# Loading v of the next attention unit at a unit's second step instead of its fifth

## The chip, the cores and the metric

One Trainium2 chip, one of its cores. The metric is the device time of one execution in microseconds (us). The engines of the core run side by side, each through its own program in order: TensorE (PE: matmuls, and PEld: their weight loads), VectorE (DVE), ScalarE (ACT), GpSimd (POOL) and SyncE (SP). SP, ACT and GpSimd also issue transfers (DMAs), which the core's 16 DMA engines carry out.

## The reference, cut to what matters

```python
def _attn_ref(q, k, v):                    # q, k, v: 4 batches x 12 heads x 448 x 64, float32
    scores = scale * np.matmul(q, k.transpose(0, 1, 3, 2)) - np.log(S)
    attn = 1.0 / (1.0 + np.exp(-scores))   # a sigmoid for each score, no softmax
    return np.matmul(attn, v)

def reference(...):
    x = attn_out.transpose(0, 2, 1, 3).reshape(B * S, H * D)     # 1792 x 768
    h = np.maximum(np.maximum(x @ w1, x @ w2), x @ w3)           # all 768 x 768
    x = h @ w_out
    g = x @ w_in;  g = np.maximum(g, 0) + alpha * np.minimum(g, 0)   # 768 x 2048
    return g @ w_out2                                            # 2048 x 768
```

## The kernel before

The kernel runs the attention first (some 140 us) and then the chain of large matrix products (the function `ff`, all of them issued by the helper on L626). The change touches the attention alone.

**Units and steps.** The function `attention` works in 12 units (`nu`), each of two pairs of heads, z = 0 and z = 1. A unit has seven steps (`NK`, c = 0 to 6). A step issues the scores of one block of 64 keys (`scores`, L506: k against q), after which ACT takes the sigmoid of them into a tile `a` (L514); and, two blocks behind, the product of that tile with v (`av`, L525), summed up in the two PSUM tiles `pav` of the unit (one for each z). The last two blocks of a unit are multiplied with v in step 0 of the next unit; then `to_x` copies the two finished `pav` out, z = 0 on ACT and z = 1 on DVE (L538). So the ACT copy of L538 comes once in a unit, at the end of the unit before.

**Getting k and q ready.** While a unit runs, the next one's k and q are turned (`turn`, called once a step: k of z = 0, k of z = 1, q of z = 0, q of z = 1). In units 1 to 11 the four calls are made at c = 1 to 4, in unit 0 at c = 3 to 6. DVE transposes the loaded rows (L487) in blocks of 32; for k it does so twice, the second time into the tile `side` (L490), and GpSimd then copies four blocks of `side` over into k's tile `kt` (L495, four copies of 32x224 for each z, eight in a unit). The scores of the next unit read `kt`. Each call ends with `load_rows`, in which SP asks for the rows that the same call of the next unit will turn (L467 for k, L474 for q: four loads for each z).

**Getting v.** `load_v` (L448) loads the v of a unit in two transfers of 224 KB, one for each z, into a tile `vt`. There are two such tiles (`bufs=2`), so the v of unit u + 1 takes the place of that of unit u - 1, and its transfer waits until the last `av` of unit u - 1 has read it. Unit 0's v is issued at the start by ACT and SP. All others are issued by GpSimd (L592), at c = 4 of the unit before: there, in GpSimd's program, they stand behind the eight copies of k of that unit (in unit 0, where the turns come later, also behind those of both z). In unit 0, GpSimd also makes a one-column copy into a tile `gate` (L497), which reads `kt`.

**Order.** Each engine's program is written out by hand in the order of the Python calls (the block runs under a manual schedule; waits between engines are put in for the data and the buffers). Between the steps `advance` lets conversions of x and of the weights onto ACT and DVE, by a planner's costs; the change does not touch it.

Of the kernel before, what the change touches and what calls it, by code (L numbers as in the profile page):

```python
# [21 lines left out]
def kernel(  # L22
# [14 lines left out]
    nc = tc.nc  # L37
# [38 lines left out]
    def slot(nm, pool="a", w=TW, dt=F32):  # L76
        if pool == "a":
            pad(pool, 48)
        t = pools[pool].tile([P, w], dt, tag="s" + pool, name=nm, bufs=room[pool])
        if pool != "a":  # L80
            pad(pool, 16)
        return t
# [38 lines left out]
    def load_half(z):  # L121
        if z >= NZ:
            return
        w, kind, m, h = halves[z]
        t = wpool.tile([P, HF, 2], U32, tag="wr", name=f"wr{z}", bufs=4)
        if kind == "col":
            nc.sync.dma_start(
                out=t.rearrange("p (k f) t -> p k (f t)", k=HK),
                in_=w[h * HF : (h + 1) * HF, 2 * m * P : 2 * (m + 1) * P].rearrange(
                    "(k p) f -> p k f", p=P  # L130
                ),
            )
        else:
            c = 2 * 32 * HK
            nc.sync.dma_start(
                out=t.rearrange("p (g f) t -> p g (f t)", g=4),
                in_=w[m * P : (m + 1) * P].rearrange("p (g f) -> p g f", g=4)[
                    :, :, h * c : (h + 1) * c
                ],
            )  # L140
        wraw[z], since[z] = t, tick[0]
# [38 lines left out]
    def advance(cols, act=None, free=False):  # L180
        now[0] += 1
        tick[0] += 1
        loads[0] = max(1, 3 * cols // STEP)
        for e in credit:
            most = cols if e == "D" else 2 * cols // 3 if act is None else act
            credit[e] = min(credit[e] + (cols if act is None else most), most)
        for todo in (urgent, flow):
            n = 0
            while n < len(todo):
                o = todo[n]  # L190
                if (
                    (free or credit.get(o.engine, loads[0] if o.engine == "L" else 1) > 0)
                    and ready(o)
                    and (o.gate is None or o.gate())
                ):
                    emit(o)
                    todo.pop(n)
                else:
                    n += 1
# [187 lines left out]
    def attention(apool, ps_s, ps_v):  # L387
# [8 lines left out]
        n = len(pairs)  # L396
# [51 lines left out]
        def load_v(u, queues):  # L448

            if u >= nu:  # L450
                return
            vts[u] = apool.tile([P, 2, NK, D], F32, tag="vt", name=f"vt{u}", bufs=2)
            for z in range(2):
                b, p = pairs[2 * u + z]
                queues[z].dma_start(
                    out=vts[u][z * KH : (z + 1) * KH].rearrange("r j c d -> r j (c d)"),
                    in_=v[b, 2 * p : 2 * p + 2].rearrange("j (r c) d -> r j (c d)", c=NK),
                )

        def load_rows(u, x, z):  # L460

            if u >= nu:
                return
            b, p = pairs[2 * u + z]
            t = raw[u, x, z] = apool.tile([P, S], F32, tag="raw", name=f"{x}r{2 * u + z}", bufs=6)
            if x == "k":
                nc.sync.dma_start(  # L467
                    out=t, in_=k[b, 2 * p : 2 * p + 2].rearrange("j (r c) d -> (j r) (c d)", c=NK)
                )
                return  # L470
            for j in range(2):
                for h in range(2):
                    p0 = j * D + 32 * h
                    nc.sync.dma_start(  # L474
                        out=t[p0 : p0 + 32].rearrange("p (n d) -> p n d", d=32),
                        in_=q[b, 2 * p + j, :, 32 * h : 32 * h + 32].rearrange(
                            "(n i) d -> i n d", i=32
                        ),
                    )

        def turn(u, x, z):

            if u >= nu:
                return
            t, r = slot(f"{x}t{2 * u + z}"), raw.pop((u, x, z))
            (keys if x == "k" else queries)[u, z] = t
            nc.vector.transpose(out=t, in_=r)  # L487
            if x == "k":
                side = apool.tile([P, S], F32, tag="side", name=f"side{2 * u + z}", bufs=2)
                nc.vector.transpose(out=side, in_=r)  # L490
                to, rows = (y.rearrange("p (c h d) -> p h c d", h=2, d=32) for y in (t, side))
                for j in range(2):
                    for h in range(2):
                        p0, p1 = j * D + 32 * h, j * D + 32 * (1 - h)
                        nc.gpsimd.tensor_copy(to[p0 : p0 + 32, 1 - h], rows[p1 : p1 + 32, h])  # L495
            if u == 1 and (x, z) == ("k", 0):
                nc.gpsimd.tensor_copy(gate[:, :1], t[:, :1])  # L497
            load_rows(u + 1, x, z)

        def scores(u, c):  # L500

            sc = ps_s.tile([P, 2, 512], F32, tag="sc", name=f"sc{u}_{c}")
            for z in range(2):
                for j in range(2):
                    r = slice(j * D, (j + 1) * D)
                    nc.tensor.matmul(  # L506
                        sc[z * KH : (z + 1) * KH, j, :S],
                        keys[u, z][r, c * KH : (c + 1) * KH],
                        queries[u, z][r],
                        start=True,  # L510
                        stop=True,
                    )
            a = at[u, c] = apool.tile([P, 2, S], F32, tag="a", name=f"a{u}_{c}", bufs=5)
            nc.scalar.activation(a, sc[:, :, :S], AF.Sigmoid, bias=bias_s, scale=scale)  # L514

        def av(u, c):

            if c == 0:
                for z in range(2):
                    pv[u, z] = ps_v.tile([P, 512], F32, tag="pv", name=f"pav{u}_{z}")  # L520
            a = at.pop((u, c))
            for z in range(2):
                r = slice(z * KH, (z + 1) * KH)
                for j in range(2):
                    nc.tensor.matmul(  # L525
                        pv[u, z][j * D : (j + 1) * D, :S],
                        vts[u][r, j, c],
                        a[r, j],
                        start=(c == 0),
                        stop=(c == NK - 1),  # L530
                    )

        def to_x(u):

            for z in range(2):
                i = 2 * u + z
                x32[i] = slot(f"x{i}")
                (nc.vector.tensor_copy if z else nc.scalar.copy)(x32[i], pv.pop((u, z))[:, :S])  # L538
                o = Op("A", 0, None, [], None, 1 if u < nu - 1 else 0)
                o.step, o.tick = now[0], tick[0]  # L540
                g, r, c = i // 12, i % 12 // 4, i // 4
                form_ops(
                    f"x{c}", i % 4, range(4 * c, 4 * c + 4), (g, r), xf,
                    lambda g, c, r: "c" if g and r == HK - 1 else "a", lambda pool: True, o,
                )
# [5 lines left out]
        gate = apool.tile([P, 64], F32, tag="gate", name="gate")  # L551
# [20 lines left out]
        for u in range(nu):  # L572
            for c in range(NK):
                scores(u, c)
                if c == 0 and u:
                    for m in (NK - 2, NK - 1):
                        av(u - 1, m)
                    to_x(u - 1)
                elif c > 1:
                    av(u, c - 2)  # L580
                if c == 1 and 1 <= u <= 4:
                    load_half(u - 1)
                if (u, c) == (2, 2):
                    with nc.allow_non_contiguous_dma(reason="a column of slopes per partition"):
                        nc.sync.dma_start(out=alpha_sb, in_=alpha.rearrange("(m p) -> p m", p=P))
                if (u, c) == (5, 0):
                    unit_ops(0, zu[0])
                n = c - (1 if u else 3)
                if 0 <= n < 4:
                    turn(u + 1, *turns[n])  # L590
                if c == 4:
                    load_v(u + 1, (nc.gpsimd, nc.gpsimd))  # L592
                if c == 0:
                    advance(1400, 800)
                elif c != 1:
                    advance(*((600, 450) if c > 2 else (1300, 450)))
# [660 lines left out]
```

## Time and profile before

| | us |
|---|---|
| median of 3 runs | 877.4 |
| lowest and highest of them | 873.63 and 878.9 |
| the profiled execution | 875.98 |
| its span, first to last instruction | 874.2 |
| PE busy in that span | 863.7 (99%) |
| DVE, ACT, POOL busy | 652.4 (75%), 525.3 (60%), 150.8 (17%) |

The profile is of one execution, whose own time is 1.8 us more than its span. A row of the timeline has the start in us from the span's start, how long it took, the engine, the line, the operation and what it writes and reads; in brackets stands how long the engine was idle before it and what it is taken to have waited for. A matmul's end is modelled, so a busy PE can still be slower than it could be; how far it got in a stretch is read from when its work was handed on.

### The profile page before, as it was taken

To read this page: it belongs to the slowest core of one execution; us is meant where nothing else is said; L and a number is where in the kernel's file an instruction comes from. 1 tells how busy PE (TensorE), PEld (TensorE's weight loads), DVE (VectorE), ACT (ScalarE), POOL (GpSimd) and SP (SyncE) were. 2 spreads that over 40 slices of the span, in tenths; PEclk is the share of its full clock that TensorE was granted. 3 is DMA by queue.
4 is the path that set the end of the run, shared out by engine and by line. 5 is a ranking of instruction groups with operands and counts; after the bars stand their busy time and mean duration, and the time that the engine had idled before them with its cause. 6 is when DMAs were issued, how large, how long until landed. Compare 5 with 4: busy or idle time off the path is not lost.

```text
span 874.2 us, 14360 instructions
## 1 busy us (share of the span) xinstructions
PE 863.7 (99%) x5044; PEld 750.9 (86%) x5044; DVE 652.4 (75%) x1261; ACT 525.3 (60%) x1022; POOL 150.8 (17%) x289
## 2 busy tenths in 40 slices
PE   9999999999999999999999999999999999999997
PEld 7645547999999999999999999999999999999997
DVE  3567875899889878787787777777868688768851
ACT  5768987656555554566656677666656655443430
POOL 2444440101101201300000122122121011001211
PEclk9999999999999999999999999999999999999999
DMA  8774740556655655732113433454455999445413
GB/s 208 164 147 110 167 93 22 153 166 219 215 139 171 203 169 140 233 121 73 37 37 104 146 130 129 161 178 157 146 176 188 368 325 365 154 146 162 133 49 64
DMA packets 137224, 137.05 MB, mean 157 GB/s; under 512 B 54752, under 2 KB 127840, under 8 KB 137152
## 3 DMA queue, kind: packets, MB, share of 16 engines
q1 hardware_dynamic: 122448, 93.24, 36.7%
q0 software_dynamic: 12416, 41.86, 14.1%
q10 hardware_dynamic: 2288, 1.03, 0.5%
q8 instruction: 40, 0.66, 0.3%
q14 instruction: 32, 0.26, 0.1%
HBM read 102.28 MB, written 33.82 MB: 156 GB/s over the span
## 4 chain that ended last, share of the span: by engine, by line
PE 92%; DMA 3%; POOL 1%; SPq 1%; DVE 1%; issue 0%; ACT 0%; POOLq 0%; DVEq 0%; ACTq 0%
PE u_0X L626 14%; PE u_1X L626 14%; PE c L626 10%; PE eW L626 10%; PE eX L626 10%; PE u_1W L626 7%; PE u_0W L626 7%; PE pav L525 5%; PE sc L506 4%; PE u_0V L626 4%; PE u_1V L626 4%; PE eV L626 3%; DMA vt<-in_v_dram 3%; POOL kt L495 1%; SPq L474 1%; DMA kr<-in_k_dram 0%
## 5 line engine op out<-in xcount | busy, mean ns | idle before, releaser
L525 PE MATMUL pav<-a,vt 64*64 64x448 f32 x672 | 116.0, 543 | 3.9 <-DMA vt<-in_v_dram 3.3
L506 PE MATMUL sc<-qt,kt 64*64 64x448 f32 x672 | 115.3, 543 | 0.0
L514 ACT ACTIVATE a<-sc,bias_s 128x896 f32<-128x896 f32 x84 | 83.2, 1009 | 24.8 <-PE sc L506 23.7
L525 PEld LDWEIGHTS pav<-a,vt 64*64 64x64 f32 x672 | 51.2, 134 | 34.8 <-issue 22.0
L506 PEld LDWEIGHTS sc<-qt,kt 64*64 64x64 f32 x672 | 52.2, 134 | 25.8 <-issue 22.3
L240 ACT ACTIVATE wt<-wr 128x384 f32<-128x384 f32 x112 | 62.2, 555 | 10.7 <-DMA wr<-in_moe_w_out_dram 9.6
L255 DVE CUSTOM_DVE_ANT_0 wt<-wr,wt 128x768 uint16<-128x768 uint16 x112 | 62.6, 559 | 3.9
L247 DVE SCALAR_TENSOR_TENSOR wr<-wr 128x384 uint32<-128x384 uint32 x112 | 62.2, 556 | 0.6
L243 ACT ACTIVATE wr<-wr 128x384 uint32<-128x384 uint32 x112 | 61.8, 552 | 0.0
L656 DVE SCALAR_TENSOR_TENSOR r<-n,nalpha,r 128x448 f32<-128x448 f32 x64 | 43.4, 682 | 24.5 <-ACT n L653 24.3
L689 POOL DMA_DIRECT2D gd<-r x48 | 26.0, 541 | 198.1 <-DVE r L656 196.9
L495 POOL COPY kt<-side 32x224 f32<-32x224 f32 x88 | 41.3, 469 | 76.6 <-DVE side L490 72.9
L1097 POOL DMA_DIRECT2D out_dram<-o x28 | 17.6, 636 | 167.7 <-DVE o L1092 167.7
L850 POOL DMA_DIRECT2D wd<-wt x32 | 17.4, 544 | 166.7 <-DVE wt L255 146.1
L246 DVE TENSOR_SCALAR wt<-wt 128x384 uint32<-128x384 uint32 x112 | 39.9, 356 | 5.5 <-ACT wt L240 5.5
L759 ACT COPY u<-u_1X 128x448 f32<-128x448 f32 x34 | 18.1, 533 | 29.9 <-PE u_1X L626 29.9
L538 DVE COPY x<-pav 128x448 f32<-128x448 f32 x12 | 7.5, 624 | 37.7 <-PE pav L525 37.7
L746 ACT COPY u_0V<-u_0X 128x448 f32<-128x448 f32 x17 | 8.8, 518 | 42.9 <-PE u_0X L626 42.9
L759 ACT COPY u<-u_0X 128x448 f32<-128x448 f32 x34 | 18.1, 533 | 27.0 <-PE u_0X L626 26.6
L811 ACT COPY y<-c 128x448 f32<-128x448 f32 x24 | 12.8, 534 | 31.6 <-PE c L626 31.6
L294 DVE TENSOR_TENSOR u<-u_0W,u 128x448 f32<-128x448 f32 x28 | 17.4, 622 | 17.3 <-ACT u L759 16.9
L294 DVE TENSOR_TENSOR u<-u_1W,u 128x448 f32<-128x448 f32 x28 | 17.5, 624 | 13.3 <-ACT u L759 8.8
(827 smaller groups left out, 2782.6 us busy)
## 6 DMA issues: line engine op xcount, KB each, us to landing
gl<-gd SPq DMA_DIRECT2D x79, 224.0 KB, 4.2
wr<-in_moe_w_out_dram SPq DMA_DIRECT2D x44, 384.0 KB, 4.2
wr<-in_moe_w_dram SPq DMA_DIRECT2D x36, 384.0 KB, 3.7
wr<-in_moe_w_in_dram SPq DMA_DIRECT2D x32, 384.0 KB, 3.6
wl<-wd SPq DMA_DIRECT2D x64, 192.0 KB, 4.1
gd<-r POOLq DMA_DIRECT2D x48, 224.0 KB, 2.3
gl_T<-gdT SPq DMA_DIRECT2D x32, 224.0 KB, 4.9
wd<-wt POOLq DMA_DIRECT2D x32, 192.0 KB, 3.9
```

The source lines that it names most:

```text
L240: nc.scalar.activation(st["T"].bitcast(F32), st["r"][:, :, 1].bitcast(F32), AF.Abs, scale=2.0**-112)
L243: nc.scalar.activation(st["r"][:, :, 0], st["r"][:, :, 0], AF.Copy, scale=2.0**-29)
L246: nc.vector.tensor_scalar(st["T"], st["T"], 3, None, ALU.logical_shift_left)
L247: nc.vector.scalar_tensor_tensor(out=st["r"][:, :, 0], in0=st["r"][:, :, 1], scalar=0x80000000, in1=st["r"][:, :, 0], op0=ALU.bitwise_and, ...
L255: nc.vector.tensor_tensor(out=st["T"], in0=st["r"][:, :, 0], in1=st["T"], op=ALU.add)
L495: nc.gpsimd.tensor_copy(to[p0 : p0 + 32, 1 - h], rows[p1 : p1 + 32, h])
L506: nc.tensor.matmul(sc[z * KH : (z + 1) * KH, j, :S], keys[u, z][r, c * KH : (c + 1) * KH], queries[u, z][r], start=True, stop=True,)
L514: nc.scalar.activation(a, sc[:, :, :S], AF.Sigmoid, bias=bias_s, scale=scale)
L525: nc.tensor.matmul(pv[u, z][j * D : (j + 1) * D, :S], vts[u][r, j, c], a[r, j], start=(c == 0), stop=(c == NK - 1),)
L626: nc.tensor.matmul(ps[:, : rh.shape[-1]], lt, rh, start=(start and z == 0), stop=(stop and z == len(mms) - 1), skip_group_check=True,)
L656: nc.vector.scalar_tensor_tensor(out=s["r"], in0=s["n"], scalar=nalpha[:, f : f + 1], in1=s["r"], op0=ALU.mult, op1=ALU.add,)
L759: nc.scalar.copy(side[g, k], banks[X][:, :TW])
```

## The change

The v of unit u + 1 is issued by GpSimd at c = 1 of unit u, in front of the turn of k of z = 0, and so in front of all of GpSimd's copies of that unit. For unit 0, the v of unit 1 is issued inside `turn`, after DVE's `side` of the first k and in front of the copies; the one-column copy into `gate` moves there with it and reads `side` instead of `kt`.

```diff
             if x == "k":
                 side = apool.tile([P, S], F32, tag="side", name=f"side{2 * u + z}", bufs=2)
                 nc.vector.transpose(out=side, in_=r)
+                if u == 1 and z == 0:
+                    nc.gpsimd.tensor_copy(gate[:, :1], side[:, :1])
+                    load_v(1, (nc.gpsimd, nc.gpsimd))
                 to, rows = (y.rearrange("p (c h d) -> p h c d", h=2, d=32) for y in (t, side))
                 for j in range(2):
                     for h in range(2):
                         p0, p1 = j * D + 32 * h, j * D + 32 * (1 - h)
                         nc.gpsimd.tensor_copy(to[p0 : p0 + 32, 1 - h], rows[p1 : p1 + 32, h])
-            if u == 1 and (x, z) == ("k", 0):
-                nc.gpsimd.tensor_copy(gate[:, :1], t[:, :1])
             load_rows(u + 1, x, z)
...
                 n = c - (1 if u else 3)
+                if u and n == 0:
+                    load_v(u + 1, (nc.gpsimd, nc.gpsimd))
                 if 0 <= n < 4:
                     turn(u + 1, *turns[n])
-                if c == 4:
-                    load_v(u + 1, (nc.gpsimd, nc.gpsimd))
```

## Rows read from the trace of the kernel before

**Rows 1.** Windows: us; busy us (x count) of PE, PEld, DVE, ACT, POOL; clock; DMA.
```profile
19.91:30.43 10.52, 10.52 (x117) 9.18 (x112) 5.03 (x9) 8.26 (x10) 4.83 (x10) 1.00 0.67 150
30.43:43.07 12.64, 11.26 (x117) 5.47 (x111) 7.72 (x13) 9.19 (x12) 4.95 (x10) 1.00 0.87 180
...
53.59:68.81 15.22, 13.41 (x120) 6.00 (x115) 7.71 (x13) 9.18 (x13) 4.94 (x10) 0.89 0.70 146
...
79.33:90.63 11.30, 11.10 (x120) 5.41 (x115) 8.86 (x17) 10.10 (x17) 4.84 (x10) 1.00 0.82 183
...
101.12:111.97 10.85, 10.81 (x118) 5.41 (x113) 8.82 (x16) 9.54 (x15) 5.30 (x10) 1.00 0.55 124
111.97:123.63 11.66, 11.22 (x120) 5.38 (x115) 9.21 (x16) 9.56 (x14) 4.94 (x10) 1.00 0.62 136
...
134.16:144.40 10.24, 10.24 (x108) 6.60 (x100) 4.01 (x7) 8.16 (x12) 0.00 (x0) 1.00 0.01 2
19.91:144.40 124.49, 120.62 (x1225) 65.73 (x1216) 83.41 (x149) 101.30 (x137) 49.60 (x100) 0.99 0.57 126
144.52:869.29 724.77, 724.77 (x3582) 671.34 (x3582) 563.22 (x1099) 413.54 (x873) 96.09 (x172) 1.00 0.50 161
```

**Rows 2.** Timeline of ACT: first and last of the twelve copies of L538.
```profile
19.91 0.53 ACT L538 COPY x<-pav 128x448 f32<-128x448 f32 x1 [0.39 <-PE pav L525]
...
144.40 0.53 ACT L538 COPY x<-pav 128x448 f32<-128x448 f32 x1 [1.07 <-PE pav L525]
```

**Rows 3.** Timeline of PE: matmuls of L525 that it stood idle for.
```profile
34.28 0.59 PE L525 MATMUL pav<-a,vt 64*64 64x448 f32 x2 [1.29 <-DMA vt<-in_v_dram]
...
56.14 0.97 PE L525 MATMUL pav<-a,vt 64*64 64x448 f32 x4 [0.59 <-DMA vt<-in_v_dram]
58.33 0.59 PE L525 MATMUL pav<-a,vt 64*64 64x448 f32 x2 [1.22 <-DMA vt<-in_v_dram]
...
114.84 0.59 PE L525 MATMUL pav<-a,vt 64*64 64x448 f32 x2 [0.44 <-DVE kt L487]
```

**Rows 4.** The chain that ended last, in unit 1: start, us, what.
```profile
25.79 0.53 POOL vt L455
26.32 7.83 DMA vt<-in_v_dram
34.15 0.14 issue
```

**Rows 5.** The tile vt: from issue to landing, all 24 transfers.
```profile
DMA to landing us min/median/max: 3.2/4.5/7.8
```

**Rows 6.** Windows, as above: the stretch at the lower clock.
```profile
59.29:62.70 3.41, 3.41 (x24) 1.37 (x18) 1.06 (x3) 1.46 (x2) 1.80 (x4) 0.50 0.68 151
```

**Rows 7.** Timeline of POOL: units 0, 1 and 8.
```profile
9.97 1.61 POOL L495 COPY kt<-side 32x224 f32<-32x224 f32 x4 [8.65 <-DVE side L490]
11.64 0.18 POOL L497 COPY gate<-kt 128x1 f32<-128x1 f32 x1
...
13.43 1.32 POOL L455 DMA_DIRECT2D vt<-in_v_dram  x2
21.74 4.05 POOL L495 COPY kt<-side 32x224 f32<-32x224 f32 x8 [6.99 <-DVE side L490]
...
104.72 4.51 POOL L495 COPY kt<-side 32x224 f32<-32x224 f32 x8 [5.60 <-DVE side L490]
```

**Rows 8.** Timeline of PE: the first scores of units 1 and 9.
```profile
17.30 1.11 PE L506 MATMUL sc<-qt,kt 64*64 64x448 f32 x8
...
109.26 0.55 PE L506 MATMUL sc<-qt,kt 64*64 64x448 f32 x2
```

**Rows 9.** DMA issues, 72.0 to 73.6 us, then 75.3 to 77.4: median us to landing.
```profile
qr<-in_q_dram SPq DMA_DIRECT2D x4, 56.0 KB, 2.1
...
qr<-in_q_dram SPq DMA_DIRECT2D x4, 56.0 KB, 5.1
```

**Rows 10.** The tile qr: waits for it, us and times.
```profile
DMA qr<-in_q_dram: 1.5, 2
```

## The prediction, made before the change was run

> **What bounds the kernel now.** I read three views in this order: the waits of PE, a table of windows by unit, and the chain of work that ended last. The table comes first here, because it says how much there is to win. The ACT copy of L538 runs when a unit's last product with v has been handed on, so its twelve starts, from 19.91 to 144.40 [rows 2], cut the attention into eleven periods, and I cut the windows there. From 144.52 to the last matmul PE is busy for 724.77 of 724.77 us [rows 1]: the matrix products behind the attention are PE's alone, without a gap, and what is won in the attention should shift them whole.
>
> An undisturbed period takes 10.52 us; the four periods that have no row share what the others leave of 124.49, which is 42.06 or 10.515 each [rows 1]. It has 14 groups of matmuls (seven of scores, seven of av), so a group takes 10.52/14 = 0.751. The last period ends with the last av instead of going on into a new unit, and has 13 groups: 9.77. Eleven periods without a stall would be 10 x 10.52 + 9.77 = 114.97. They take 124.49 [rows 1]. So **9.5 us** of the attention are lost, and they lie in few periods: 12.64 - 10.52 = 2.12, then 15.22 - 10.52 = 4.70, then 0.78, 0.33, 1.14, and 10.24 - 9.77 = 0.47 in the last.
>
> What they are lost to is seen at PE. Its waits stand at the first av of a unit, and they are for v: 1.29 us before 34.28, then 0.59 and 1.22 in the unit of the 15.22 [rows 3]. The wait of 0.44 before 114.84 is put down to a transpose, but it stands at the same place, the second half of the first av, and I take it for v too. Listed idle time is less than the loss, because a wait for one half of v lets the matmuls of the other half run on alone: PE counts as busy and gets less done. The chain shows why v is late [rows 4]: GpSimd issues it at 25.79 and 26.32, behind its copies of k which began at 21.74 [rows 7]; it takes 7.83 us to land, and PE starts 0.14 after that. So a unit's first av is bound by copies of k, the issue of v, and the landing.
>
> One part of the 4.70 is not a wait: the granted clock is 0.50 from 59.29 to 62.70, that is 1.2 GHz instead of 2.4 [rows 6], right behind the two waits of that unit. Work done at half speed for 3.41 us is some 1.7 us late.
>
> **The change, part by part.**
>
> *v for units 2 to 11, moved to c = 1.* Its two transfers now stand ahead of the eight copies. They still wait for the buffer, which the last av of the unit before frees; that is where the ACT copy of L538 begins, 19.91 in unit 1 [rows 2]. Issuing the pair takes 1.32 in the one row shown [rows 7], so it would be out by 19.91 + 1.3 = 21.2, where it is now begun at 25.79: 5.9 us earlier at its start. The slowest landing of all 24 is 7.83, the median 4.5 [rows 5]. From 20.6, the start of the second transfer, the slowest gives 28.4; the next period begins at 30.43 and av needs v after that. So even the slowest landing has two us to spare, and I cost the wait for v at nothing: 5.9 us more lead hides it. The gain is the whole loss of 9.5, if nothing else is as late.
>
> *What is queued behind it on GpSimd.* The copies of k. They are held by DVE's `side`, not by GpSimd: in unit 1 they begin at 21.74 after 6.99 us idle [rows 7], 1.83 after the period's start. The pair takes 1.32 of that 1.83 and is gone before the copies could begin. In unit 8 they begin at 104.72, 3.6 after the period's start of 101.12. So the cost is nothing as long as the buffer is free within 0.5 us of the ACT copy. If it were freed at the copies' old start instead, each unit's copies would come 1.3 later; that is the upper bound, and it is one of the rivals.
>
> *What is late next.* The copies of k, for the scores of the next unit. In unit 8 they end at 104.72 + 4.51 = 109.23, and the first scores of unit 9 stand at 109.26 [rows 7, 8]: just in time. Without the stall of that period (0.33) those scores would want to start 0.33 sooner. Its bounds are 0 (the copies move with the period, since `side` hangs on the copy of `pav` on DVE) and 0.33. I take 0.3, because the copies start on `side` whether PE stalled behind that point or not.
>
> *v of unit 1, inside `turn`.* Now: four copies from 9.97, the gate copy of 0.18, four more copies, the v pair from 13.43 [rows 7]. Changed: gate copy and pair go first, so the copies end 1.32 + 0.18 = 1.5 us later, at about 13.5 + 1.5 = 15.0. The first scores of unit 1 start at 17.30 [rows 8]: 2.3 us of cover. Without that cover it would cost its 1.5 once. v itself was no one's wait there, so nothing is won.
>
> *DMAs behind the moved ones.* The same bytes go out. But v is now ahead of the q loads of its unit instead of in their midst. Loads of q land in 2.1 us without v beside them and in 5.1 with it [rows 9], so being passed costs a load at most some 3 us. In the whole attention DVE waits for q twice, 1.5 us in all [rows 10], and the scores of unit 1 at 17.30 hide that. From unit 1 on q and k are asked for a unit before they are turned. I cost it at nothing; the other bound is those 3 us once, in unit 0, against no more cover than the copies have there, 2.3: 0.7.
>
> Here a rule speaks against the change. The Trainium skill (DMA: Bandwidth & Descriptors, "Issuing engines are not separate DMA queues") says that transfers from SP, ACT and GpSimd share the same 16 engines and interleave, so a v issued earlier takes from q and k what it gains. The trace agrees that they disturb each other (2.1 against 5.1); what it adds is that the disturbed ones are not awaited.
>
> *The clock.* The fall to 0.50 stands in the one unit with two long waits. With these gone I expect it not to come, and its 1.7 us are part of the 9.5. If it comes anyway, 1.7 stay.
>
> **The sum.** 9.5 lost, less 0.3 that the copies of k may keep: 9.2. Against the profiled execution's own 875.98 that is 875.98 - 9.2 = **866.8**. The median of the runs, 877.4, lies 1.4 higher. I don't carry those 1.4 over: the products behind the attention have no gap in which runs could differ, so runs probably differ in the very stalls that go. If they were carried over it would be 868.2.
>
> **The rivals.**
>
> *B: the copies of k become the bound.* For it: the 0.03 us between copies and scores in unit 8. Against: undisturbed periods exist in the second half too, with the same eight copies, so there the copies are in time for 10.52. If the last six units lose 0.5 each, 3.0 stay: 866.8 + 3.0 = 869.8.
>
> *C: the half-clock stretch comes anyway.* For it: it began behind waits of only 1.22 us, so it may need little. Against: no other such stretch stands in the attention between 19.91 and 144.40 (that window's clock is 0.99 by this one alone). 866.8 + 1.7 = 868.5. The Trainium skill (TensorE: Matmul & The Clock Gate, Part 1) has activity release a throttle that is otherwise the default; by that rule, too, a PE without waits keeps its clock, and the trace agrees in the undisturbed periods (1.00).
>
> *D: the change does nothing.* If the DMA engines are what makes v late, an earlier issue only waits longer. For it: DMA engines are busy 0.87 in the period of the 12.64. Against: they are busy 0.70 in the period that loses most and 0.67 in one that loses nothing [rows 1], and the lead grows by 5.9 us, more than any period loses. Then about 875, within 1%.
>
> *E: GpSimd's wait holds up k (slower).* The v pair now waits for PE in front of the copies. If the buffer were freed so late that the pair ended well after `side`, the copies and then the next scores would be late in unit after unit. It decides once the pair ends later than the 1.83 after the period's start plus what the copies have in hand. With the pair starting only as the copies would have begun, each of the ten units that wait for a buffer loses its 1.32: 866.8 + 13.2 = 880.0, some 0.5% slower; slower by over 1% needs (9.2 + 8.8)/10 = 1.8 a unit. Against: what frees the buffer is the end of the same matmuls that the ACT copy waits for, 1.83 earlier, or for the half of z = 1 a little behind it.
>
> **How the numbers follow.** Forecast 0.62, B 0.15, C 0.08, D 0.08, E 0.07. The forecast's own range is 865.5 (nothing kept, and a little from halves that no longer run apart) to 868.5. With B and C it reaches 870.8 at the upper end, and I take 865 to 871.5: D and E, 0.15 together, are left out. 1% is 8.8 us, about what a measurement of this kernel can tell from no change. The forecast is beyond that by 0.4 counted from the profiled execution and by 1.8 from the median, so I give it 0.52 of its 0.62 as faster by over 1%; of C half, 0.04. E passes 1% on its side with 0.03. So faster 0.56, within 1% 0.41, slower 0.03.
>
> **What would show it.** Right: GpSimd's v pair begins within half a us of the ACT copy of L538 in every unit, with k's copies behind it at the same distance from that copy as before; no wait of PE for vt; eleven periods in 115 to 115.5 us; no row of 0.50 inside the attention; the products behind it still 724.8 us long. Wrong: v pairs that end after `side` (E), scores that wait for `kt` (B), v landing after the next period's start (D). What would upset the forecast most is a wait of PE on something that its stall for v now covers.

## The result and the profile after

| | before | changed |
|---|---|---|
| median of 6 runs, us | 876.36 | 867.13 |
| lowest and highest | 873.63, 878.94 | 866.45, 868.87 |
| the profiled execution and its span | 875.98, 874.2 | 868.87, 867.1 |

The ratio is 0.9895, with a 95% interval of 0.9871 to 0.992: 1.05% faster. The kernel is faster beyond the noise, but the interval lies on both sides of 1%, so it stays open whether by more than 1%. Line numbers of the changed kernel are one to three higher: L507 are the scores, L526 the products with v, L539 the copies of `pav`, L498 GpSimd's copies of k.

Windows of the changed kernel, cut again at the ACT copies of `pav` (us; busy us and count of PE, PEld, DVE, ACT, POOL; clock; DMA):

```profile
22.04:32.56 10.52, 10.52 (x116) 9.16 (x112) 5.03 (x9) 8.26 (x10) 4.88 (x10) 1.00 0.75 151
32.56:43.09 10.53, 10.53 (x117) 9.16 (x112) 7.56 (x13) 9.20 (x13) 5.00 (x10) 1.00 0.82 188
53.61:64.13 10.52, 10.52 (x116) 9.16 (x112) 7.56 (x13) 9.19 (x12) 5.00 (x10) 1.00 0.66 156
95.70:106.23 10.53, 10.53 (x117) 9.12 (x112) 8.83 (x16) 9.51 (x14) 5.35 (x10) 1.00 0.66 155
127.27:137.04 9.77, 9.77 (x106) 7.50 (x97) 4.01 (x7) 8.06 (x11) 0.00 (x0) 1.00 0.00 0
22.04:137.04 115.00, 115.00 (x1225) 98.15 (x1217) 83.21 (x149) 101.01 (x137) 50.09 (x100) 1.00 0.57 134
137.04:861.81 724.77, 724.77 (x3583) 671.38 (x3582) 563.83 (x1099) 413.93 (x873) 95.96 (x172) 1.00 0.50 161
```

They answer to [rows 1]. The periods that took 12.64 and 15.22 take 10.53 and 10.52, and the last one takes the 9.77 that 13 groups need. All eleven take 115.00, where 114.97 was worked out for no stall at all; they took 124.49. The products behind them take 724.77 in both.

GpSimd's timeline in the changed kernel, units 0, 1 and 8:

```profile
12.01 0.18 POOL L492 COPY gate<-side 128x1 f32<-128x1 f32 x1 [10.70 <-DVE side L490]
12.13 1.33 POOL L455 DMA_DIRECT2D vt<-in_v_dram  x2
13.51 3.25 POOL L498 COPY kt<-side 32x224 f32<-32x224 f32 x8
22.36 1.18 POOL L455 DMA_DIRECT2D vt<-in_v_dram  x2 [5.60 <-PE pav L526]
23.87 4.05 POOL L498 COPY kt<-side 32x224 f32<-32x224 f32 x8 [0.33 <-DVE side L490]
...
96.03 1.18 POOL L455 DMA_DIRECT2D vt<-in_v_dram  x2 [3.55 <-PE pav L526]
99.07 4.51 POOL L498 COPY kt<-side 32x224 f32<-32x224 f32 x8 [1.87 <-DVE side L490]
```

These answer to [rows 7]. v is issued 0.3 us after the ACT copy (22.36 against 22.04, 96.03 against 95.70), the copies of k still wait for DVE's `side` behind it, and PE waits for nothing of the attention any more. The whole list of PE's waits in the execution is:

```profile
PE warm L568 <- DVE zeros L551: 1.2, 1, 1.2
PE turn_q L428 <- DMA kqn<-in_q_dram: 0.7, 1, 0.7
```

The profiled execution is the longest of the six, and yet no stall is in it. It lost 2.13 us before the first period began: the first ACT copy stands at 22.04, before at 19.91 [rows 2]. So its sum is 875.98 - 9.49 (124.49 to 115.00) + 2.13 at the start + 0.25 in what follows the last ACT copy (867.1 - 137.04 = 730.06 against 874.2 - 144.40 = 729.8) = 868.87, which is its time. The start is taken up in the last section.

### The profile page after: what moved, and what is told of

It reads as the page before. It is cut to its first block, busy times and chain, and to the rows that moved or that the text cites. A ratio compares the mean times of both kernels' runs of the same rounds, so it can differ in the third digit from the quotient of the medians.

```text
span 867.1 us, 14358 instructions
## 1 busy us (share of the span) xinstructions
PE 859.9 (99%) x5044; PEld 785.2 (91%) x5044; DVE 652.6 (75%) x1261; ACT 525.3 (61%) x1022; POOL 151.1 (17%) x289
## 2 busy tenths in 40 slices
DMA packets 137223, 137.04 MB, mean 158 GB/s; under 512 B 54752, under 2 KB 127840, under 8 KB 137152
## 4 chain that ended last, share of the span: by engine, by line
PE 99%; DMA 0%; DVE 0%; issue 0%
PE u_0X L627 14%; PE u_1X L627 14%; PE c L627 10%; PE eW L627 10%; PE eX L627 10%; PE sc L507 7%; PE pav L526 7%; PE u_1W L627 7%; PE u_0W L627 7%; PE u_0V L627 4%; PE u_1V L627 4%; PE eV L627 3%; DMA kqn<-in_q_dram 0%; PE turn_q L428 0%; PE turn_k L428 0%; DVE o L1093 0%
## 5 line engine op out<-in xcount | busy, mean ns | idle before, releaser
L507 PE MATMUL sc<-qt,kt 64*64 64x448 f32 x672 | 88.6, 536 | 0.0
L526 PE MATMUL pav<-a,vt 64*64 64x448 f32 x672 | 88.3, 536 | 0.0
L507 PEld LDWEIGHTS sc<-qt,kt 64*64 64x64 f32 x672 | 54.3, 133 | 8.8 <-issue 0.5
L526 PEld LDWEIGHTS pav<-a,vt 64*64 64x64 f32 x672 | 53.4, 133 | 9.8 <-ACT a L515 2.1
L498 POOL COPY kt<-side 32x224 f32<-32x224 f32 x88 | 41.3, 469 | 14.3 <-DVE side L490 10.5
L539 DVE COPY x<-pav 128x448 f32<-128x448 f32 x12 | 7.5, 624 | 35.4 <-PE pav L526 35.4
```

The costliest lines, as they stand in the source:

```text
L507: nc.tensor.matmul(sc[z * KH : (z + 1) * KH, j, :S], keys[u, z][r, c * KH : (c + 1) * KH], queries[u, z][r], start=True, stop=True,)
L526: nc.tensor.matmul(pv[u, z][j * D : (j + 1) * D, :S], vts[u][r, j, c], a[r, j], start=(c == 0), stop=(c == NK - 1),)
```

## The experiments

In the diffs, lines are against the kernel named. Losses in the attention are counted as in the prediction: the eleven periods between the twelve ACT copies, less 114.97.

### Each half alone

Only the move to the second step, against the kernel before:

```diff
-                if c == 4:
-                    load_v(u + 1, (nc.gpsimd, nc.gpsimd))
+                if not u and c == 4:
+                    load_v(1, (nc.gpsimd, nc.gpsimd))
...
                 n = c - (1 if u else 3)
+                if u and n == 0:
+                    load_v(u + 1, (nc.gpsimd, nc.gpsimd))
```

> The move to the second step alone, for v of units 2 to 11; v of unit 1 is issued as before, behind the copies of k. Theory (all of the gain comes from the stalls of units 2 to 11): as the changed kernel, 866 to 868 us, ratio about 0.9895, and ten full periods of 10.5 us between the ACT copies of pav. Rival (getting v of unit 1 out earlier is part of the gain, because it clears the queues for the later loads): 869 us or more, with a wait for vt left in one of units 1 to 3.

868.08 us, ratio 0.991 (0.9882 to 0.9939): just past the theory's 866 to 868, and not to be told from the changed kernel. All its eleven periods:

```profile
20.96:135.97 115.01, 115.01 (x1226) 81.18 (x1217) 83.55 (x149) 101.34 (x137) 50.37 (x100) 1.00 0.58 135
```

Nothing is lost in the attention, and PE waits for v nowhere, so the rival falls. This half alone takes all the stalls away.

Only the edit in `turn` (v of unit 1 in front of the copies of k), against the changed kernel:

```diff
-                if u and n == 0:
-                    load_v(u + 1, (nc.gpsimd, nc.gpsimd))
                 if 0 <= n < 4:
                     turn(u + 1, *turns[n])
+                if u and c == 4:
+                    load_v(u + 1, (nc.gpsimd, nc.gpsimd))
```

> The other half of the change alone: v of unit 1 in front of the copies of k, all later v at the fifth step behind the copies. Theory: nothing is won, ratio 0.998 to 1.002, about 876 us, with 8 to 11 us lost in the eleven periods and PE waits for vt in units 2, 4 and 9; copies of k of unit 0 end 1.5 us later than in the kernel before and nothing waits for them. Rival: 2 us or more are won. It is also a second look at the stalls of the kernel before: if the half-clock stretch comes from the two waits in unit 4, it should be there when those waits are, and not elsewhere.

874.91 us, ratio 0.9976 (0.9953 to 0.9999). That is 2.08 us less than the kernel before in the same session (876.99), just the rival's 2 us, but the interval reaches almost to no change. Its attention and its two periods that correspond to 15.22 and 12.64:

```profile
21.65:142.85 121.20, 118.01 (x1224) 66.84 (x1216) 83.45 (x149) 101.29 (x137) 49.42 (x100) 1.00 0.59 132
53.37:66.77 13.40, 11.71 (x120) 5.50 (x115) 7.71 (x13) 9.19 (x14) 4.95 (x10) 1.00 0.79 172
32.17:42.85 10.68, 10.68 (x115) 7.27 (x111) 7.57 (x13) 9.20 (x13) 4.95 (x10) 1.00 0.81 148
```

6.2 us are lost, not 9.5; the theory had 8 to 11. Of the difference, 1.82 is in the unit of the 15.22, where the same two waits come again without the fall of the clock:

```profile
55.77 0.97 PE L526 MATMUL pav<-a,vt 64*64 64x448 f32 x4 [0.44 <-ACT a L515]
57.98 0.59 PE L526 MATMUL pav<-a,vt 64*64 64x448 f32 x2 [1.24 <-DVE qt L487]
```

The profile puts these two down to ACT and DVE, but they too are for v: the two transfers of this unit's v, issued at 50.3 and 50.8, land after 5.4 and 7.0 us, at 55.7 and 57.8, just before PE goes on.

```profile
DMA to landing us min/median/max: 5.4/6.2/7.0
```

The period's clock is 1.00. And 1.96 is in the unit of the 12.64, whose v landed within 6.1 us, before within 7.8. (The other units lose 0.5 more than before.) Whether the earlier v of unit 1 did that, by leaving less in the queues, or the execution, isn't settled by one profile. For the changed kernel it doesn't matter: with the first half in place there is no stall left for this one to remove.

### v between the two lots of copies

Against the changed kernel:

```diff
-                if u and n == 0:
+                if u and n == 1:
                     load_v(u + 1, (nc.gpsimd, nc.gpsimd))
```

> As the changed kernel, but v of units 2 to 11 is issued between the copies of k of z = 0 and those of z = 1, so 3.5 to 6 us after the start of the period instead of at it. Theory of lead (all that counts is that a landing of 4.5 us, at worst 7.8, ends before the first av of the next unit, some 11.7 us after the period's start): the median landing is still in time, so 867 to 869 us, with at most one or two short waits for vt. Rival (v must stand in front of all copies, or GpSimd is the bound): about half of the 9 us comes back, 871 to 872 us.

870.81 us, ratio 0.9938 (0.9917 to 0.9958): between the two ranges. By the medians some 3.7 of the 9 us come back. The profiled execution, one of its shorter ones (869.4), lost 1.94 us in the attention. In units 1 to 7 it lost nothing, and PE waits for v nowhere, so the lead is enough. The rest is in the last units, 1.22 of it in unit 8. GpSimd and PE there:

```profile
97.38 2.31 POOL L498 COPY kt<-side 32x224 f32<-32x224 f32 x4 [5.86 <-DVE side L490]
99.64 1.18 POOL L455 DMA_DIRECT2D vt<-in_v_dram  x2
100.86 2.50 POOL L498 COPY kt<-side 32x224 f32<-32x224 f32 x4
...
103.41 0.59 PE L507 MATMUL sc<-qt,kt 64*64 64x448 f32 x1 [0.46 <-POOL kt L498]
```

The v pair has pushed the second lot of copies back by its 1.2 us; they end at 103.36, and the scores that wait for them start at 103.41. What counts is not only how early v goes out, but what it holds up: the pair is free only in the gap in which GpSimd waits for `side`.

### How much the copies of k have in hand

Against the changed kernel, the same copy made twice:

```diff
-                        nc.gpsimd.tensor_copy(to[p0 : p0 + 32, 1 - h], rows[p1 : p1 + 32, h])
+                        for _ in range(2 if u > 1 and z == 0 else 1):
+                            nc.gpsimd.tensor_copy(to[p0 : p0 + 32, 1 - h], rows[p1 : p1 + 32, h])
```

> The changed kernel with the four copies of k of z = 0 made twice (same data) in units 1 to 10, so that the copies of k end 1.6 to 2.3 us later. It measures how much the copies have in hand. Theory (they are the next bound, and in hand is the time from their end to the first scores of the next unit: about 2 us in units 1, 2 and 4, 1 or less in the others, nearly nothing in unit 8): unit 8 loses 2 us, units 3, 5, 7, 9 and 10 lose 0.5 to 1 each, units 1, 2, 4 and 6 nothing; 4 to 6 us in all, so 871 to 873. Rival (the copies are well hidden and only what is issued behind them was late): 867 to 868 us.

877.48 us, ratio 1.001 (0.9982 to 1.0039): the whole gain is gone, about twice what was expected. All periods, then that of unit 8, and its copies with the scores that wait for them:

```profile
21.85:147.22 125.37, 123.11 (x1224) 79.00 (x1216) 85.98 (x149) 101.04 (x137) 70.62 (x140) 1.00 0.53 124
100.21:112.81 12.60, 12.15 (x120) 6.70 (x116) 8.98 (x16) 9.48 (x14) 7.32 (x14) 1.00 0.51 120
```
```profile
104.06 6.74 POOL L499 COPY kt<-side 32x224 f32<-32x224 f32 x12 [1.87 <-DVE side L490]
```
```profile
110.01 1.43 PE L508 MATMUL sc<-qt,kt 64*64 64x448 f32 x3 [0.45 <-POOL kt L499]
```

10.4 us are lost. GpSimd is busy 70.6 us there instead of 50.1, about 2 us more in each of ten units. Units 1 and 2 lose nothing, units 3 to 7 lose 0.5 to 1.4 each, units 8 and 9 lose 2.1 and 1.9, nearly the whole of it, and unit 10 loses 1.3. The theory holds in kind and was too low in size: units 4 and 6, which were to lose nothing, lose 0.5 and 0.8, and unit 9 about twice what it was given. Only in units 8 and 9 have the copies almost nothing in hand.

### What made v land late

Three edits of the kernel before, none of which moves v. First alpha, 2048 elements of 4 bytes. The program has its load in unit 2; in the kernel before SP issues it at 26.77, just behind the v that unit 2 needs:

```diff
-                if (u, c) == (2, 2):
+                if (u, c) == (9, 6):
                     with nc.allow_non_contiguous_dma(reason="a column of slopes per partition"):
                         nc.sync.dma_start(out=alpha_sb, in_=alpha.rearrange("(m p) -> p m", p=P))
```

> The kernel before, with the load of alpha (2048 elements of 4 bytes, issued just behind v in unit 2) moved from unit 2 to unit 9. Theory of a crowded queue (the 7.8 us landing of the v that unit 2 needs is that load's doing): that landing falls to about 4.5 us, the period of unit 2 from 12.6 to 11.0 us or less, the whole to about 874.5 us. Rival (being issued behind the copies is enough to be late): the period stays at 12 us or more and the whole at 876 us.

879.17 us, ratio 1.002 (0.9992 to 1.0048), so the theory falls (it had 874.5). The chain of waits in unit 1 has the same shape as in [rows 4]:

```profile
28.11 0.53 POOL vt L455
28.64 7.94 DMA vt<-in_v_dram
36.58 0.14 issue
```

v takes 7.94 us to land without alpha beside it. Its period takes 14.41 instead of 12.64, because here the clock fell in this unit and not in that of the 15.22, which takes 13.73 at full clock (a window of the fall, and the two periods):

```profile
32.76:47.17 14.41, 12.78 (x116) 5.76 (x111) 7.71 (x13) 9.19 (x12) 4.94 (x10) 0.88 0.69 159
57.69:71.42 13.73, 11.70 (x120) 5.34 (x115) 7.71 (x13) 9.18 (x14) 4.95 (x10) 1.00 0.76 166
36.68:40.08 3.40, 3.37 (x20) 1.45 (x24) 1.98 (x4) 0.02 (x1) 3.05 (x6) 0.50 0.67 108
```

Then the weights, 384 KB which SP issues in units 1 to 4 in front of the next k:

```diff
-                if c == 1 and 1 <= u <= 4:
+                if c == 3 and 1 <= u <= 4:
                     load_half(u - 1)
```

> The kernel before, with the 384 KB of weights that SP issues in units 1 to 4 right in front of the next k (and within 0.1 us of v in units 1 and 4) issued behind k instead, two steps later in the program. Theory (v is late because it is behind the copies, and lands in 6 to 8 us instead of 4.5 where it meets these weights): the landings of the pairs issued in units 1 and 4... that is, for units 2 and 4, fall below 6 us, the periods of 12.6 and 15.2 shrink by 1 us or more each, the whole to 873 to 875 us. Rival (the q loads in front of v set its landing, the weights don't matter): landings of 7 to 8 us stay and the whole stays at 876 to 877.

872.61 us, ratio 0.9962 (0.9937 to 0.9987), a little better than the theory's 873 to 875. The attention and the periods of units 2 and 4 are:

```profile
20.07:140.58 120.51, 117.94 (x1224) 63.46 (x1216) 83.36 (x149) 101.24 (x138) 49.54 (x100) 1.00 0.58 131
30.59:42.71 12.12, 11.01 (x116) 5.78 (x111) 7.71 (x13) 9.19 (x13) 4.94 (x10) 1.00 0.89 204
53.23:64.96 11.73, 10.84 (x120) 5.26 (x115) 7.65 (x13) 9.17 (x13) 4.94 (x10) 1.00 0.79 186
```

and the landings of the v that they need, first that for unit 2 (issued in unit 1), then that for unit 4 (issued in unit 3):

```profile
DMA to landing us min/median/max: 5.3/6.3/7.3
...
DMA to landing us min/median/max: 4.1/4.7/5.3
```

For unit 4 the weights were part of the crowd: the landing falls from 7.1 to 5.3 at most, and the period to 11.73, which is 1.7 less than the 13.40 that this unit takes at full clock with the weights in front (in the half-change above). For unit 2 the landing falls little, from 7.8 to 7.3, and the period by 0.5, so there the theory misses. Then both edits together, that of alpha and that of the weights:

> The kernel before with both edits together: the weights of units 1 to 4 behind k, and the load of alpha in unit 9. Theory (either of the two next to v is enough to make it land late, which is why moving alpha alone did nothing and moving the weights alone left 7.3 us in unit 2): the pair for unit 2 lands in less than 5.5 us, the period of unit 2 falls to 11 us or less, the whole to about 871. Rival (the loads of q and k around v, which stay, make it late): the landing for unit 2 stays at 7 us, its period at 12, the whole at 872 to 873.

873.63 us, ratio 0.997 (0.9951 to 0.9989): more than either theory gave, and no better than the weights alone. The attention, the period of unit 2, and the landing for it:

```profile
20.14:141.35 121.21, 119.06 (x1225) 64.63 (x1216) 83.40 (x149) 101.21 (x137) 49.53 (x100) 1.00 0.59 130
30.67:41.89 11.22, 11.00 (x116) 5.77 (x111) 7.65 (x13) 9.17 (x12) 4.94 (x10) 1.00 0.78 167
```
```profile
DMA to landing us min/median/max: 5.1/5.8/6.4
```

The landing still takes 6.4, between the theory's 5.5 and the rival's 7, with the loads of q and k around it. So no single transfer makes v late: neighbours set whether it lands in 4 us or in 8. Thinning the queue brings units 2 and 4 from 6.8 us lost (1.7 of it the clock) to 2.1, not to nothing, and the other 4.1 of the 6.2 lost in this execution (121.21 - 114.97) lie in units 6 to 11, where no load was taken out of the way of v. Being issued behind the copies is what all these kernels share, and of the edits made only those that moved v in front of them took the loss to zero.

### A longer warm-up

Against the changed kernel:

```diff
-        for _ in range(6):
+        for _ in range(8):
```

These are the warm-up matmuls on `zeros`. It was tried because the start was taken to be what is left of the differences among runs.

> The changed kernel with eight warm-up matmuls at the start instead of six, which bridge the 0.7 us that PE idles before the first turns. In the profiles so far the clock reaches 1.00 at 4.6 to 9.4 us after the start and the first scores come at 7.9 to 10.3 us accordingly; this is the spread that is left among runs of the changed kernel. Theory (idling in front of the turns puts the rise off): the first scores come at 8 us, the median falls by 1 us to about 866. Rival (when the clock rises depends on the moment the run begins, not on that gap): 867 us as before, with the same spread, or 0.3 us more for the longer warm-up.

867.34 us, ratio 0.9896 (0.9859 to 0.9933), with six runs from 866.82 to 867.83: the same time as the changed kernel. PE no longer waits in front of the turns, and the first scores came at 8.57 in its profiled execution. Nothing is won, and the theory that the gap before the turns puts the clock off isn't borne out; one profile can't say what sets it.

## Why the prediction was right

**The loss and its place.** 9.5 us were to be won in the attention, none behind it. 124.49 - 115.00 = 9.49 were won in the profiled execution, and the products behind take 724.77 in both. Counting the periods was the step that carried the forecast: the waits for v that the profile lists, 3.3 us in four places, are a third of what they cost.

**The issue of v hides in GpSimd's wait for `side`.** Foretold: within half a us of the ACT copy, with the pair gone before `side` is there. Measured: 0.3 us behind the copy, and 0.3 us to spare in the tightest units (the pair runs from 22.36 to 23.54, the copies begin at 23.87). Rival E is excluded by this. In these units (1, 2 and 4) a later pair would first eat up what the copies have in hand, by e5 some 2 us. In unit 8, where the copies have nothing in hand, the pair has 1.87 us to spare.

**The landings.** The longest of the changed kernel takes 6.7 us and is one of the first two, at the start; those issued at the second step take 3.1 to 4.9 and are in time by several us. Two things came together here, an earlier issue and a shorter landing (before up to 7.8). The earlier issue alone would have done: the second transfer of unit 1 starts at 22.95, and 7.83 more is 30.8, before the period's end at 32.56. Rival D, that the change does nothing, falls with them. Its premise is partly true: what else is queued makes v later. But of the edits to the queue that of alpha wins nothing and the other two win 2 to 4 us, where the move wins 9.

**The copies of k.** 0.3 us was set aside for them, and none was lost: this term was too high. The reason given, that the copies don't move when the stall goes, was wrong. In unit 8 they begin 99.07 - 95.70 = 3.37 after the ACT copy, before 104.72 - 101.12 = 3.60; the two halves of `pav` now end together, so DVE's copy of the second, from which `side` follows, comes sooner after the first: 0.06 us after the ACT copy of 95.70, before 0.29 after that of 101.12. The rows are DVE's copy before and after, then the first scores of unit 9 after:

```profile
101.41 0.62 DVE L538 COPY x<-pav 128x448 f32<-128x448 f32 x1 [2.07 <-PE pav L525]
95.76 0.62 DVE L539 COPY x<-pav 128x448 f32<-128x448 f32 x1 [1.95 <-PE pav L526]
103.62 1.11 PE L507 MATMUL sc<-qt,kt 64*64 64x448 f32 x8
```

The copies of unit 8 end at 99.07 + 4.51 = 103.58, again just in time. As the next bound (rival B) the copies were named rightly; e5 shows how near it is: about 2 us more of copies in each of ten units cost 10.4 us in all.

**The clock.** The fall did not come in the changed kernel, as foretold, nor in the profiles of the kernels that keep the move or nearly so (e1, e3, e5, e7). But the prediction took it for a fixed consequence of two long waits. It isn't: the half-change alone had the same two waits (0.44 and 1.24) at a clock of 1.00, and the kernel with alpha moved had its fall in another unit. So 1.7 of the 9.5 belonged to that execution, and the medians hold such falls only in part. The record has the mean granted clock of every execution: 0.998 or more in the profiles without a fall in the attention, 0.997 in the two with one. Of the 62 executions of the kernel before that ran beside the experiments, 22 have 0.997 or less, with a median of 879.4 us; the other 40 have a median of 875.5. Of the 18 executions of the three kernels in which PE waits for nothing in the attention (the changed one, e1, e7), none has 0.997 or less. That fits waits being what lets the fall happen; why it comes in one execution and not in another stays open.

**Loads of q.** Foretold at nothing: DVE waits for q nowhere in the changed kernel, before 1.5 us in two places [rows 10].

**The median.** 866.8 against 867.13, and 9.2 us less against 9.23 by the medians. So near a meeting is partly luck: 0.3 was kept for copies that kept nothing, and the start, which the prediction left out, differs by 2.13 between the two profiled executions. The 1.4 us between the profiled execution and the median of before weren't carried over, on the argument that runs differ only in the stalls that go. Half of that was missed: the runs of the changed kernel still spread by 2.4 us, and its start alone cost the profiled execution 2.13. Without the start's part, that execution would have been at 866.7. Of the prediction's figures, the 870.8 for B and C has no working: 866.8 + 3.0 + 1.7 is 871.5, the end of its range. And 1% is not what a measurement here can just tell from no change: the interval is a quarter of a per cent to each side.

## What to carry to other kernels

An issue of a transfer stands in its engine's program like any other work; put it where that engine waits for something anyway, in front of the work that it would else stand behind, and count what fits into that gap: here 1.2 us of issuing into 1.5 us of waiting, and the same pair 3 to 6 us further on, between the copies, cost some 3.7 us again. Measure the loss by the distance between landmarks that come once a period, not by the idle time listed: half-late data lets a part of the engine run on, so it counts as busy. And before a stall is called removed, look at what stands next in line, since with the stall gone the copies of k are at the very edge in unit 8.

## What the runs showed of the hardware that was not expected

**The start.** The first turns of PE took 1.76 us where they take 1.00 in other executions, in the changed kernel as follows:

```profile
4.67 1.76 PE L428 MATMUL turn_q<-ident,kqn 128*64 128x64 f32 x28 [0.70 <-DMA kqn<-in_q_dram]
6.18 1.74 PE L428 MATMUL turn_k<-ident,kqn 128*64 128x64 f32 x28
7.68 1.65 PE L428 MATMUL turn_q<-ident,kqn 128*64 128x64 f32 x28
9.14 1.00 PE L428 MATMUL turn_k<-ident,kqn 128*64 128x64 f32 x28
10.07 1.45 PE L507 MATMUL sc<-qt,kt 64*64 64x448 f32 x10
```

and with v between the copies, the third and a later row of the same stretch:

```profile
6.25 1.01 PE L428 MATMUL turn_q<-ident,kqn 128*64 128x64 f32 x28
8.00 2.95 PE L507 MATMUL sc<-qt,kt 64*64 64x448 f32 x24
```

The same instructions behind the same warm-up reach full pace at some 4.6 us in one execution and at 9.1 in another, and the first scores come at 8.0 or at 10.07. No edit explains it: the first thing that the change moves runs at 12.01. I take it for the clock coming up at another moment, from the durations, since the trace holds no granted clock before that moment; this is not shown. It is 2 us of noise in any single execution, as much as several of the effects looked for here.

**The fall of the clock in the attention** (0.50 for 3.4 us, some 1.7 us lost) came behind waits of 1.2 to 1.6 us, with PE busy again at once, in two of the profiled executions, and in another, the half-change's, it did not come behind waits of 0.44 and 1.24. By their mean clock some third of the executions of the kernel before (22 of 62) seem to have had one or more; they are some 4 us longer, which is more than one fall costs.
